# A new order of the first pieces, and short matmuls of zeros on TensorE, in a fused cross-attention and maxout kernel

## The chip, the core and the metric

The kernel runs on one core of a Trainium2 chip. Five engines take part: TensorE (PE in the profile; its weight loads are listed apart as PEld) multiplies matrices and writes only to PSUM, an on-chip memory of eight banks; VectorE (DVE), ScalarE (ACT) and GpSimd (POOL) do casts, copies, exponentials and sums; SyncE (SP) issues nearly all transfers between HBM and the on-chip memory SBUF, which then run on 16 DMA engines. Every engine works through its own instructions in the order in which they were written, and waits where an operand or a buffer is not ready. The metric is the device time of one execution in microseconds (us).

## The reference

`x` is (8, 8, 512, 64): batch, head, row, depth. `state` is (8, 8, 32, 64). Both are read in float32.

```python
scores = scale * x @ state^T;    a  = softmax(scores);   xread = a @ state
scores2 = scale * state @ x^T;   a2 = softmax(scores2);  sread = a2 @ x
y = concatenate([xread, sread], axis=rows)       # heads side by side: (8*544, 512)
out = maximum(y @ w1, y @ w2) @ w_out            # w1, w2: 512x1024, w_out: 1024x512
```

The output is (4352, 512) in float32.

## The kernel before

The kernel writes the maximum as `y @ w2 + relu(y @ (w1 - w2))`. For a batch b the matrix `y` is `a` times a block-diagonal state, so the weights are first multiplied with the state of the batch: `sw` = state times `wd = w1 - w2` (columns 0 to 1023) and state times `wwo = w2 @ w_out` (columns `w`). Then, for each batch,

- `l1.b.f` (line 332): two matmuls give 128 of the 1024 hidden columns, `re` takes the maximum with zero (lines 325, 327);
- `l2.b.c.q` (line 346): for each of four row groups c the hidden columns of the quarter q (two f) are multiplied with `w_out`; `l2.b.c.o` (line 341) adds the part by `wwo`; `le` copies the sum out and `store` writes it.

Before this come, for a batch: the load of `x` in two halves (`ldx.b.g`, 512 KB each), casts to bfloat16 (`ce`, `cb`), the transposes of `x` (on PE `xt`, copied out of PSUM by `xte`; for later batches by a transposing transfer, `xtd`), the scores `sc` (line 240), their exponential `exp` (line 248, on ACT), the sums `red` (line 252), the division `mul` (line 256), the transposes of `a` (on PE `at`, copied by `ate`; later by the transfer `atd`), and the reading of the state by x, `sr`, `sre`, `srt`, `srte` (line 280). `S` transposes the state (loads `ldS`, cast `cS`, copies `Se`; for batches 2 to 7 by the transfer `Sd` after the masked casts `mS`).

The weights are loaded in pieces, `ldw1.k`, `ldw2.k` and `ldwo.q`. A piece k of w1 and w2 is a range of columns and of 128-row tiles, listed in `PIECES`: all are 512 KB. `cw2` casts a piece of w2, `w2` transposes it on PE (line 405), `w2e` copies it out of PSUM; `sub.k.h` subtracts half of a piece of w2 from w1 (line 417); `cwo` casts a piece of `w_out`. `ww.i.q` (line 460) accumulates `wwo` for the row tile i over the column quarter q, and `wwe` copies it out. `CHUNKS[b]` says in which column ranges `sw` is made for the batches 0 and 1.

Until the loop over the batches 2 to 6 begins (line 573), the order on every engine is the list `ORDER`, written out by hand token by token. `name>V`, `>A`, `>P` put a token on DVE, ACT or POOL; `name@i` or `@i,j` puts a PE token into the PSUM bank i. A token with neither is a transfer, issued by SP (the state of batch 0, `ldS.0.1`, by ACT). `idle.9@0` is nine matmuls of zeros (line 426). PE's tokens up to the loop hold batches 0 and 1 whole, and the scores and `sw` of batch 2. In the loop, `cast_b(b+2)` on POOL and `xt_dma(b+2)` on SP stand ahead of the division `mul` and `at_dma` of batch b+1; `RELEASE` gives the order in which the loop takes over the banks. A buffer `big[k]` holds in turn the pieces and batches that `slot` lists: `x4` takes the place of the left half of w2.

```python
PIECES = [(0, 512, 0, 2), (0, 512, 2, 4), (512, 1024, 0, 2), (512, 1024, 2, 4)]   # columns, row tiles
```

## Time and profile before

| | |
|---|---|
| time, three runs | median 151.17 us (151.1 to 151.3) |
| the profiled execution | 150.94 us, its span 149.0 us |
| mean clock granted to TensorE | 0.989 |
| busy: PE, DVE, ACT, POOL | 138.1, 83.3, 66.1, 53.0 us |
| moved by DMA | 29.44 MB, mean 198 GB/s |
| PE's share of the chain that ended last | 81%, DMA 10% |

How to read the rows that follow. A row of the timeline or of the chain of waits begins with its start and its length in us from the start of the span, then the engine, the line of the program, the operation, what it writes and reads, and how many instructions were merged (x8); in brackets stands how long the engine was idle before and what it waited for. In a row of the view by stretches stand the stretch, its length, and for PE, PEld, DVE, ACT and POOL the busy time with the number of instructions; then the clock granted to PE, the mean share of the DMA engines, and GB/s. Rows on SPq are transfers being issued; the length is the issue, not the transfer. In the two rows of slices each digit is the busy share, or the clock, in tenths for a fortieth of the span.

### The profile page before, as it was taken

To read this page: it belongs to the slowest core of one execution; us is meant where nothing else is said; L and a number is where in the kernel's file an instruction comes from. 1 tells how busy PE (TensorE), PEld (TensorE's weight loads), DVE (VectorE), ACT (ScalarE), POOL (GpSimd) and SP (SyncE) were. 2 spreads that over 40 slices of the span, in tenths; PEclk is the share of its full clock that TensorE was granted. 3 is DMA by queue.
4 is the path that set the end of the run, shared out by engine and by line. 5 is a ranking of instruction groups with operands and counts; after the bars stand their busy time and mean duration, and the time that the engine had idled before them with its cause. 6 is when DMAs were issued, how large, how long until landed. Compare 5 with 4: busy or idle time off the path is not lost.

```text
span 149.0 us, 3067 instructions
## 1 busy us (share of the span) xinstructions
PE 138.1 (93%) x1205; PEld 68.9 (46%) x1224; DVE 83.3 (56%) x163; ACT 66.1 (44%) x120; POOL 53.0 (36%) x81
## 2 busy tenths in 40 slices
PE   6846979999999999999999999999999999999990
...
PEclk9987999999999999999999999999999999999999
...
GB/s 137 255 396 362 370 387 378 283 342 93 189 246 200 106 248 297 129 208 230 235 145 290 234 114 189 264 282 145 70 31 255 7 66 141 145 0 96 115 140 80
DMA packets 36063, 29.44 MB, mean 198 GB/s; under 512 B 23120, under 2 KB 31568, under 8 KB 35152
## 3 DMA queue, kind: packets, MB, share of 16 engines
...
q10 hardware_dynamic: 272, 0.07, 0.2%
...
## 4 chain that ended last, share of the span: by engine, by line
PE 81%; DMA 10%; SPq 3%; DVE 1%; issue 1%; POOL 1%; ACT 0%
PE bank L346 38%; PE bank L332 17%; PE bank L341 9%; DMA big<-in_moe_w_out_dram 7%; PE bank L309 4%; PE bank L460 3%; DMA big<-in_x_dram 3%; SPq L155 3%; PE bank L365 2%; PE bank L375 2%; PE bank L240 2%; PE bank L280 1%; PE bank L373 1%; DVE wd L417 1%; POOL wo L103 1%
## 5 line engine op out<-in xcount | busy, mean ns | idle before, releaser
L346 PE MATMUL bank<-wo,r 128*128 128x512 bf16 (+1 forms) x259 | 61.4, 372 | 0.5
L346 PEld LDWEIGHTS <-r 128*128 128x128 bf16 x264 | 25.4, 98 | 28.5 <-issue 0.3
L99 ACT COPY big<-bank 128x512 f32<-128x512 f32 (+1 forms) x17 | 9.7, 573 | 47.1 <-PE bank L346 47.1
L332 PE MATMUL bank<-at,sw 128*128 128x512 bf16 x126 | 30.0, 379 | 0.1
L256 POOL TENSOR_TENSOR a<-e,er 128x512 bf16<-128x512 bf16 x16 | 16.7, 1065 | 36.3 <-ACT e L248 16.0
L327 DVE TENSOR_SCALAR r<-bank 128x512 bf16<-128x512 f32 x29 | 20.0, 691 | 15.9 <-PE bank L332 15.5
L325 ACT ACTIVATE r<-bank 128x512 bf16<-128x512 f32 x35 | 21.2, 608 | 8.2 <-PE bank L332 8.0
L101 DVE CAST sw<-bank 128x512 bf16<-128x512 f32 x24 | 15.3, 685 | 9.4 <-PE bank L309 9.3
L103 POOL CAST xe<-big 128x512 bf16<-128x512 f32 x28 | 16.4, 620 | 10.0 <-DMA big<-in_x_dram 10.0
L332 PEld LDWEIGHTS <-sw 128*128 128x128 bf16 x128 | 12.0, 98 | 14.0 <-issue 0.2
L101 DVE COPY big<-bank 128x512 f32<-128x512 f32 (+1 forms) x16 | 10.5, 654 | 13.6 <-PE bank L346 11.2
L341 PE MATMUL bank<-sw,at 128*128 128x512 bf16 (+1 forms) x56 | 17.1, 372 | 0.3
L103 POOL CAST xb<-big 128x1024 bf16<-128x1024 f32 x12 | 12.3, 1041 | 12.1 <-issue 11.4
L252 DVE TENSOR_REDUCE sums<-e 128x16 f32<-128x512 bf16 x16 | 10.6, 664 | 4.5 <-ACT e L248 4.4
L99 ACT CAST sw<-bank 128x512 bf16<-128x512 f32 x24 | 12.7, 599 | 0.2
L248 ACT ACTIVATE e<-bank 128x512 bf16<-128x512 f32 x16 | 9.0, 595 | 4.9 <-PE bank L240 4.5
L460 PE MATMUL bank<-wo,w2m 128*128 128x512 bf16 x30 | 7.8, 379 | 1.9 <-ACT w2m L99 1.2
L341 PEld LDWEIGHTS <-at 128*128 128x128 bf16 x66 | 5.7, 97 | 5.3
L240 PEld LDWEIGHTS <-xt 128*128 128x128 bf16 x128 | 5.1, 98 | 2.6 <-DVE xt L101 0.7
L240 PE MATMUL bank<-sbd,xt 128*128 128x64 bf16 x128 | 5.5, 193 | 0.6 <-DVE xt L101 0.6
L309 PE MATMUL bank<-wd,sbd 64*32 64x512 bf16 x128 | 5.8, 382 | 0.3 <-DVE sbd L101 0.2
L101 DVE COPY w2m<-bank 128x1024 bf16<-128x1024 bf16 (+1 forms) x4 | 2.8, 689 | 5.1 <-PE bank L375 4.1
...
## 6 DMA issues: line engine op xcount, KB each, us to landing
big<-in_x_dram SPq DMA_DIRECT2D x14, 512.0 KB, 5.1
...
big<-in_moe_w_dram SPq DMA_DIRECT2D x8, 512.0 KB, 10.2
big<-in_moe_w_out_dram SPq DMA_DIRECT2D x4, 512.0 KB, 10.3
...
out_dram<-big SPq DMA_DIRECT2D x1, 512.0 KB, 2.6
...
```

The costliest lines, as they stand in the source:

```text
L99: nc.scalar.copy(o, i)
L101: nc.vector.tensor_copy(o, i)
L103: nc.gpsimd.tensor_copy(o, i)
L240: nc.tensor.matmul(pv[:, c, kk], xt_s[b % 2][:, c, k, :], sbd[:, b, k, :], start=(c == 0 and kk == 0), stop=(c == NC - 1 and kk == 1))
L256: (nc.gpsimd if eng == "P" else nc.vector).tensor_mul(e_view(a_s[b % 2], hh), e_view(e_s[b % 2], hh), er_s[b % 2][:, hh].unsqueeze(3).to_b ...
L309: nc.tensor.matmul(pg[g][32 * i:32 * i + 32, 0:n], sbd[64 * g:64 * g + 64, b, i, 32 * g:32 * g + 32], rhs, start=True, stop=True)
L325: nc.scalar.activation(out=o, in_=p, func=ACTF.Relu)
L327: nc.vector.tensor_scalar(o, p, scalar1=0.0, scalar2=None, op0=ALU.max)
L332: nc.tensor.matmul(p, sw_s[b % 3][:, g, f * 128:(f + 1) * 128], at_s[b % 3][:, g].rearrange("p c t -> p (c t)"), start=(g == 0), stop=(g = ...
L341: nc.tensor.matmul(p[:, lo:hi], at_s[b % 3][:, g, c, :], sw_s[b % 3][:, g, FF + lo:FF + hi], start=(start and g == 0), stop=(stop and g == 1))
L346: nc.tensor.matmul(p[:, lo:hi], r_s[b % 2][:, f, c * 128:(c + 1) * 128], wo[:, f, lo:hi], start=(start and j == 0), stop=(stop and j == le ...
L460: nc.tensor.matmul(p, w2t[:, f, i, :], wo[:, f, :], start=(first and f % 2 == 0), stop=(last and f % 2 == 1))
```

## The change

The new `PIECES` cuts the left half of w1 and w2 into two column quarters with all four row tiles, in place of two halves of the row tiles; the right half keeps its two pieces. `CHUNKS` for batch 0 makes `sw` in three ranges. The loads come in the order: state of batch 1, x0, x1 (right half of the heads first), w2.0, w1.0, wo.0, w2.3, w2.1, wo.1, w1.1, wo.2, wo.3, w2.2, w1.2, w1.3, then x2, x3.1, the state of batches 2 to 7, x4.1, x3.0. The transfers `xtd.3` and `ldx.4.0` stand behind `atd.2`. The remaining tokens of `ORDER` are put in another order, with other engines and banks in places, to go with these loads. `idle` takes a width; a new token `fill.n@i` is one matmul of zeros with 256 columns. There are 24 of them, and `idle.9` stands behind `xt.1.0`. `RELEASE` follows the new banks. What is computed stays the same.

```diff
--- before.py
+++ after.py
@@ -16,40 +16,42 @@
 
 
 
-PIECES = [(0, 512, 0, 2), (0, 512, 2, 4), (512, 1024, 0, 2), (512, 1024, 2, 4)]
-
-CHUNKS = [[(0, 512), (512, 1024)], [(0, 512), (512, 1024)]]
+PIECES = [(0, 256, 0, 4), (256, 512, 0, 4), (512, 1024, 0, 2), (512, 1024, 2, 4)]
+
+CHUNKS = [[(0, 256), (256, 512), (512, 1024)], [(0, 512), (512, 1024)]]
 
 ORDER = """
-ldx.0.0 ldS.0.1 idle.9@0 ldx.0.1 ldw2.2 ldw2.3 ldwo.3 ldw1.3 ldw1.2 ldS.1.2 ce.0.0>V ce.0.1>P ldx.1.1 cS.0.1>V ldx.1.0
-S.0.1@0 xt.0.0@1 Se.0.1.0>V Se.0.1.1>A ce.0.2>P ce.0.3>A xte.0.0>V xt.0.1@0 ldwo.2 sc.0.0@1 xte.0.1>V exp.0.0>A
-cw2.2>P ldw2.1 sc.0.1@0 red.0.0>V exp.0.1>A w2.2@1 mul.0.0>P cw2.3>A sr.0@0 red.0.1>V ldw2.0 mul.0.1>P sre.0>V w2.3@2
-cwo.3>A ldwo.0 w2e.2>V srt.0@0 at.0.0@3 srte.0>A sub.3.0>V w2e.3>A ldwo.1 sub.3.1>V ldw1.0 ate.0.0>A ww.2.3@2
-sub.2.0>V ldw1.1 at.0.1@1 cS.1.2>A ww.3.3@3 ww.1.3@0 sub.2.1>V ate.0.1>A ldS.2.8 S.1.2@4 sw.0.1@1,5 Se.1.2.1>V
-ce.1.3>A Se.1.2.0>V ce.1.2>P sw.1.1@4,6 swe.0.1.1>V ww.0.3@7 swe.0.1.0>A swe.1.1.0>V xt.1.1@5 swe.1.1.1>A ce.1.1>P
-l1.0.7@1 ce.1.0>A xte.1.1>V l1.0.4@6 l1.0.6@4 re.0.7>A re.0.4>V cwo.2>P xt.1.0@5 re.0.6>A sc.1.1@1 l1.0.5@6 xte.1.0>V
-exp.1.1>A ww.3.2@3 re.0.5>A sc.1.0@1 red.1.1>V ww.1.2@0 exp.1.0>A ww.2.2@2 cw2.1>V ww.0.2@7 l2.0.1.2@1 mul.1.1>P
-ldx.3.1 red.1.0>V w2.1@6 cw2.0>A l2.0.2.2@5 mul.1.0>P w2e.1>V l2.0.2.3@5 l2.0.1.3@1 cwo.0>V w2.0@6 at.1.1@4 ww.2.0@2
-w2e.0>V ldx.2.1 ww.3.0@3 cwo.1>P ate.1.1>V ww.0.0@7 ww.1.0@0 sub.0.1>V ldx.2.0 ww.3.1@3 at.1.0@4 ldx.3.0 sub.0.0>V
-ww.0.1@7 wwe.3>A ww.1.1@0 sub.1.1>P ate.1.0>V wwe.0>A ww.2.1@2 wwe.1>V l1.1.7@7 wwe.2>A sr.1@4 sub.1.0>V re.1.7>A
-sw.0.w@2,0 sre.1>V sw.0.0@3,6 swe.0.w.1>A l1.1.5@7 swe.0.w.0>V l1.1.6@4 swe.0.0.1>A mS.1>P l1.1.4@0 re.1.5>A re.1.6>V
-l2.0.0.2@6 re.1.4>A l2.0.1.o@1 swe.0.0.0>V ce.3.2>P sw.1.0@4,7 mS.0>A sw.1.w@3,0 ce.3.3>P swe.1.0.1>V l2.0.0.3@6
-swe.1.w.1>A cb.3.1>P Sd l1.0.0@2 swe.1.0.0>V l1.0.1@7 swe.1.w.0>A re.0.0>V l2.0.3.2@4 cb.2.1>P re.0.1>A l2.0.2.o@5
-l1.1.1@2 ce.3.0>P l2.0.1.0@1 re.1.1>V l1.0.2@7 cb.2.0>P l1.1.3@3 re.0.2>V l2.0.3.o@4 re.1.3>A ce.3.1>P xtd.2 l1.1.0@2
-ce.2.1>P l2.0.3.0@4 re.1.0>A srt.1@3 l2.0.0.0@6 ldx.4.0 cb.3.0>P srte.1>V l1.0.3@2 l2.0.0.o@6 re.0.3>A ce.2.2>P
-l2.0.3.3@4 xtd.3 l1.1.2@2 ce.2.0>P l2.0.1.1@1 re.1.2>A ce.2.3>P l2.1.3.2@3 le.0.1>V l2.1.3.3@3 l2.1.3.1@3 l2.1.3.0@3
-l2.1.2.2@1 ldx.4.1 l2.1.0.o@2 sc.2.1@7 l2.0.3.1@4 exp.2.1>A sc.2.0@0 l2.0.0.1@6 exp.2.0>A red.2.1>V l2.1.0.0@2
-le.0.3>A l2.1.0.3@2 red.2.0>V mul.2.1>P l2.1.0.2@2 l2.1.2.3@1 le.0.0>V l2.1.2.o@1 mul.2.0>P l2.1.0.1@2 l2.0.2.0@5
-le.1.0>A atd.2 l2.1.2.1@1 l2.0.2.1@5 l2.1.3.o@3 le.0.2>A l2.1.2.0@1 le.1.3>V sw.2.1@5,2 store.0 le.1.2>A sw.2.0@6,4
-swe.2.1.0>V sw.2.w@3,0 swe.2.1.1>A sr.2@1 swe.2.0.0>V l2.1.1.3@5 swe.2.w.1>A l2.1.1.o@5 sre.2>V swe.2.0.1>A l2.1.1.2@5
-l2.1.1.1@5 swe.2.w.0>V srt.2@1 l2.1.1.0@5 srte.2>V le.1.1>A
+ldS.1.2 ldS.0.1 fill.18@0 ldx.0.0 fill.12@1 fill.11@0 ldx.0.1 fill.14@1 fill.21@0 fill.16@1 ldx.1.1 fill.10@0 fill.5@1
+ldx.1.0 fill.2@0 fill.7@1 fill.4@0 ldw2.0 cS.1.2>P ldw1.0 cS.0.1>V S.0.1@0 fill.15@1 fill.0@2 Se.0.1.1>V Se.0.1.0>A
+fill.23@1 ce.0.1>A ce.0.0>P ldwo.0 fill.19@2 fill.20@1 xt.0.0@2 ldw2.3 ce.0.2>V ce.0.3>A ldw2.1 S.1.2@1 Se.1.2.0>A
+Se.1.2.1>V xt.0.1@0 xte.0.0>A fill.22@1 xte.0.1>V ldwo.1 ce.1.2>P ce.1.3>A sc.0.1@0 ldw1.1 fill.17@2 fill.1@1 xt.1.1@3
+exp.0.1>A fill.3@1 sc.0.0@2 xte.1.1>V ce.1.1>A ce.1.0>P exp.0.0>A red.0.1>V sc.1.1@3 fill.6@1 ldwo.2 xt.1.0@0
+exp.1.1>A idle.9@1 red.0.0>V mul.0.1>P ldwo.3 xte.1.0>A ldw2.2 mul.0.0>V cw2.0>A sub.0.0>P red.1.1>V sc.1.0@0 fill.9@1
+ldw1.2 exp.1.0>A w2.0@3 at.0.0@1 sub.0.1>V at.0.1@0 w2e.0>A sr.1@2 cwo.0>P ldw1.3 red.1.0>V sw.0.0@4,5 sr.0@6
+ate.0.1>A ldx.2.1 fill.8@3 swe.0.0.0>A swe.0.0.1>V mul.1.0>P ww.0.0@0 cw2.3>A ate.0.0>V ww.2.0@5 sre.0>V l1.0.0@1
+mul.1.1>P ww.1.0@4 cw2.1>A re.0.0>V l1.0.1@6 ldx.2.0 at.1.1@3 sre.1>V re.0.1>A w2.1@1 cwo.1>P ww.3.0@7 ate.1.1>A
+w2e.1>V ldx.3.1 w2.3@2 at.1.0@3 ww.1.1@4 sub.1.1>V w2e.3>A srt.1@1 ww.3.1@7 sub.1.0>V ww.0.1@0 ate.1.0>A ww.2.1@5
+cwo.2>V srte.1>A sw.0.1@3,2 ldS.2.8 sw.1.0@1,6 swe.0.1.1>A ww.3.2@7 swe.1.0.1>V swe.0.1.0>A l2.0.0.0@2 cwo.3>P
+swe.1.0.0>A l1.0.2@6 l1.0.3@1 re.0.2>A ww.2.3@5 cw2.2>V re.0.3>A ww.3.3@7 w2.2@6 wwe.3>V ww.2.2@5 w2e.2>A l1.1.2@1
+sub.2.0>V l1.1.0@7 sub.2.1>V re.1.2>A l1.1.3@6 ww.0.3@0 re.1.3>A re.1.0>V l1.1.1@1 wwe.2>A ww.1.2@4 sub.3.1>V ldx.4.1
+ww.0.2@0 re.1.1>A sub.3.0>V ww.1.3@4 wwe.0>A l2.1.2.1@1 wwe.1>V ce.2.3>P sw.0.2@5,7 ldx.3.0 sw.1.1@0,6 cb.2.1>P
+swe.0.2.1>V swe.0.2.0>A sw.1.w@4,3 l2.1.2.0@1 swe.1.1.1>A swe.1.1.0>V srt.0@7 cb.2.0>P l1.0.5@5 swe.1.w.0>A l1.0.4@6
+swe.1.w.1>V l1.1.6@0 srte.0>A ce.2.0>P xtd.2 re.0.4>A re.0.5>V l2.0.3.0@7 ce.3.2>P l2.1.1.o@3 re.1.6>A sw.0.w@5,6
+ce.3.3>P l1.1.4@0 swe.0.w.1>A swe.0.w.0>V mS.1>P l1.1.5@4 re.1.4>V mS.0>A l1.1.7@5 l2.0.3.1@7 re.1.5>V re.1.7>A
+l1.0.7@0 l2.0.2.2@6 re.0.7>A cb.3.1>P Sd l2.1.0.2@5 l2.1.2.2@1 l2.0.2.0@6 ce.2.1>P l2.1.2.3@1 ce.3.0>P l1.0.6@0
+ce.3.1>P l2.1.2.o@1 re.0.6>A l2.0.2.o@6 le.1.2>V cb.3.0>P l2.0.2.1@6 l2.0.1.3@0 ce.2.2>P l2.0.3.2@7 l2.1.0.o@5
+l2.0.0.1@2 l2.0.0.3@2 l2.0.3.o@7 l2.1.1.0@3 l2.0.0.2@2 sc.2.1@1 l2.1.1.3@3 exp.2.1>A sc.2.0@4 l2.0.3.3@7 exp.2.0>A
+red.2.1>V l2.0.2.3@6 le.0.3>A l2.0.1.1@0 red.2.0>V mul.2.1>P l2.0.0.o@2 le.0.2>A l2.1.3.3@7 le.0.0>A l2.1.1.2@3
+mul.2.0>P sr.2@6 l2.1.0.1@5 sre.2>V atd.2 l2.1.3.2@7 l2.0.1.o@0 l2.1.1.1@3 xtd.3 l2.1.0.0@5 le.1.1>A l2.1.0.3@5
+l2.1.3.o@7 le.1.0>A sw.2.0@3,6 sw.2.1@2,4 ldx.4.0 swe.2.0.1>V sw.2.w@5,1 swe.2.1.0>A l2.0.1.2@0 swe.2.1.1>V l2.1.3.0@7
+swe.2.w.0>A l2.1.3.1@7 swe.2.w.1>A swe.2.0.0>V srt.2@5 l2.0.1.0@0 le.1.3>A srte.2>V le.0.1>V store.0
 """
 
 LATE = 2
 
 WHOLE = (7,)
 
-RELEASE = [7, 2, 6, 0, 4, 3, 1, 5]
+RELEASE = [6, 2, 4, 1, 3, 5, 7, 0]
 
 
 @with_exitstack
@@ -420,10 +422,10 @@
     def wo_cast(q, eng):
         copy(eng, wo[:, 2 * q:2 * q + 2, :], half("o", q // 2)[:, q % 2 * 2:q % 2 * 2 + 2, :])
 
-    def idle(n, ring):
+    def idle(n, ring, w=512):
         p = bank(ring)
         for j in range(n):
-            nc.tensor.matmul(p, wz[:, 0:128], wz, start=True, stop=True)
+            nc.tensor.matmul(p[:, 0:w], wz[:, 0:128], wz[:, 0:w], start=True, stop=True)
 
     nc.vector.memset(wz, 0.0)
     nc.vector.memset(ones, 1.0)
@@ -479,7 +481,7 @@
         sre=("sr", lambda p, b, e: sr_ev(p, b)), srte=("srt", sr_cp), re=("l1", l1_ev), w2e=("w2", w2_ev))
     oth = dict(
         ldS=load_s, ldx=load_x, ldw2=lambda k: load_w(2, moe_w2, k), ldw1=lambda k: load_w(1, moe_w1, k), ldwo=load_wo,
-        idle=idle, cS=s_cast, mS=lambda z, e: s_mask(z, LATE, B, e), Sd=lambda: s_dma(LATE, B), ce=cast_e, cb=cast_b, xtd=xt_dma,
+        idle=idle, fill=lambda k, r: idle(1, r, 256), cS=s_cast, mS=lambda z, e: s_mask(z, LATE, B, e), Sd=lambda: s_dma(LATE, B), ce=cast_e, cb=cast_b, xtd=xt_dma,
         atd=at_dma, red=lambda b, h, e: red(b, h), mul=mul, cw2=w2_cast, sub=w_sub, cwo=wo_cast, ww=ww_mm, l2=l2_mm,
         wwe=lambda i, e: copy(e, wwo[:, i, :], open_[f"ww{i}"]), le=lambda b, c, e: l2_out(b, c, open_[f"l2{b}{c}"], e),
         Se=lambda lo, hi, j, e: s_ev(done[f"S.{lo}.{hi}"], lo, hi, j, e), store=store,
```

## The prediction

> **What bounds the kernel now.** The page first, its busy time and its slices:
>
> ```profile
> PE 138.1 (93%) x1205; PEld 68.9 (46%) x1224; DVE 83.3 (56%) x163; ACT 66.1 (44%) x120; POOL 53.0 (36%) x81
> PE   6846979999999999999999999999999999999990
> PEclk9987999999999999999999999999999999999999
> ```
>
> TensorE (PE) is busy for 93% of the span; its slices are below nine tenths only in five of the first six and in the last, and its clock dips to 7 in the fourth. Then the view by stretches, and from the timeline the first `l1` group of the loop over the batches:
>
> ```profile
> 31.30:54.66 23.36, 23.03 (x184) 10.63 (x188) 12.53 (x27) 11.96 (x21) 13.29 (x17) 1.00 0.80 205
> 54.66:149.00 94.34, 89.75 (x757) 44.17 (x767) 49.35 (x97) 37.40 (x72) 25.37 (x32) 1.00 0.59 154
> ```
> ```profile
> 54.66 3.62 PE L332 MATMUL bank<-at,sw 128*128 128x512 bf16 x16
> ```
>
> From 54.66 on PE is busy 89.75 of 94.34 us, so I let the loop take the same time whenever it starts. The question is when PE gets there. The chain of waits gives the price of each kind of PE work when nothing waits.
>
> ```profile
> 23.86 0.45 PE bank L405 x8
> 52.06 0.36 PE bank L280 x32
> 58.28 0.47 PE bank L240 x16
> 68.67 3.45 PE bank L332 x16
> 76.91 0.77 PE bank L309 x24
> ```
>
> ORDER holds 144 matmuls of 512 columns (32 `ww`, 32 `l1`, 80 `l2`) at 3.45/16, 31.05 us; 87 transposes at 0.45/8, 4.9; 48 score matmuls at 0.47/16, 1.4; three `sr` at 0.36, 1.1; 72 `sw` matmuls at 0.77/24, 2.3. Sum 40.8. So PE loses 54.66 - 40.8 = 13.9 us before the loop, and the change can gain only in those. By 17.0 it has done 45 transposes (2.5), two score groups (0.5), one `sr`, two `sw` (0.5) and five matmuls of `ww` (1.1), together 4.9: 12.1 us are lost up to there, 1.8 after.
>
> What is late at first are the loads: the first instruction that uses a piece starts when it has landed.
>
> ```profile
> 4.50 0.43 DVE L101 CAST xe<-big 128x512 bf16<-128x512 f32 x1 [2.21 <-DMA big<-in_x_dram]
> 4.84 0.70 DVE L101 CAST sb<-sf 128x256 bf16<-128x256 f32 x1
> 6.21 0.61 POOL L103 CAST xe<-big 128x512 bf16<-128x512 f32 x1 [0.82 <-DMA big<-in_x_dram]
> 9.13 1.04 POOL L103 CAST wb<-big 128x1024 bf16<-128x1024 f32 x1 [2.30 <-DMA big<-in_moe_w_dram]
> 10.43 1.05 ACT L99 CAST wb<-big 128x1024 bf16<-128x1024 f32 x1 [0.90 <-DMA big<-in_moe_w_dram]
> 16.32 0.61 POOL L103 CAST xe<-big 128x512 bf16<-128x512 f32 x1 [4.13 <-DMA big<-in_x_dram]
> 18.86 0.61 POOL L103 CAST xe<-big 128x512 bf16<-128x512 f32 x1 [1.93 <-DMA big<-in_x_dram]
> 20.21 1.04 POOL L103 CAST wo<-big 128x1024 bf16<-128x1024 f32 x1 [0.74 <-DMA big<-in_moe_w_out_dram]
> 28.50 1.26 POOL L417 TENSOR_TENSOR wd<-big,big 128x512 bf16<-128x512 f32 x1 [1.82 <-DMA big<-in_moe_w_dram]
> ```
>
> The same view cut finer gives, at the end of each row, the clock that PE was granted, the DMA share and the GB/s moved:
>
> ```profile
> 0.00:3.04 3.04, 1.77 (x5) 0.67 (x6) 1.19 (x3) 1.49 (x2) 1.52 (x20) 1.00 0.32 83
> 3.04:6.45 3.41, 3.10 (x15) 1.37 (x14) 1.26 (x3) 0.17 (x1) 1.03 (x2) 1.00 1.00 292
> 6.45:9.86 3.41, 1.70 (x28) 1.12 (x26) 2.62 (x5) 1.90 (x4) 1.11 (x2) 1.00 0.96 339
> 9.86:13.27 3.41, 3.04 (x53) 2.46 (x53) 1.95 (x7) 2.40 (x4) 2.33 (x3) 0.50 1.06 389
> 13.27:16.68 3.41, 2.01 (x23) 1.05 (x24) 3.03 (x7) 2.84 (x6) 0.36 (x1) 1.00 1.10 348
> 17.00:18.00 1.00, 1.00 (x19) 0.76 (x12) 0.85 (x2) 0.88 (x2) 0.00 (x0) 1.00 1.05 382
> ```
>
> **The change part by part.** *Loads.* Most pieces are 512 KB, and the bytes up to the last weight are the same in both orders, so I let the k-th piece land when the k-th landed before. Between the rows I go by equal steps: 1.47 for the four from 10.43 to 16.32, 1.38 for the six from 20.21 to 28.50. On SP the small state load of batch 1 now goes ahead of x0, one issue of 0.4 to 0.5 us: x0 at 4.9 and 6.4. Then x1 near 9.25 and 10.6 (it came at 16.3 and 18.8), w2.0 11.9, w1.0 13.4, wo.0 14.8, w2.3 16.3, w2.1 18.8, wo.1 20.2, w1.1 21.6, wo.2 23.0, wo.3 24.3, w2.2 25.7, w1.2 27.1, w1.3 28.5. The quarter pieces move runs of 1 KB, as x does, in place of 2 KB. No row times such a W load; by the rates just shown, 382 GB/s while x1 was on its way, 348 to 389 ahead of it, four pieces of 0.52 MB could differ by 0.6 us. I take 0 (382 is nearest), and keep 0.6 for the range; a gain has no reason.
>
> *Zeros.* `idle.9` goes from the head to behind `xt.1.0`; 24 `fill`s of 256 columns come in, 11 ahead of `S.0.1`. The nine are one row of the timeline now:
>
> ```profile
> 1.27 4.02 PE L426 MATMUL bank<-wz 128*128 128x512 bf16 x9 [1.27 <-DVE ones L429]
> ```
>
> The nine zeros took 0.43 each against 0.216 later, so PE began at half rate though the clock column says 1.00. By the rows cut finer PE is granted half from 9.86 to 13.27, after 3.41 us with 1.70 busy, and full again after 3.04 busy; 2.01 busy kept it. A fill thus costs 0.21 at half rate, 0.11 at full. The 11 run from 1.27 to 3.6; PE then waits for the cast of S0, now first on DVE: 4.7 to 5.4 (it began at 4.84, behind x0's cast). From 5.5 on five fills, then `xt.0.0`, `S.1.2` and `xt.0.1` at half rate (0.9, 0.2, 0.9) with a fill, then the scores keep it about 70% busy, so I take full rate from about 10, ahead of `idle.9`. The fills end before the inputs of what stands behind them are there, and cost nothing. Only `idle.9` is near: from 12.6, 9 x 0.216 bring it to 14.55, while `w2.0` waits for its cast until 14.9. Without that cover the nine would cost 1.9, at half rate 3.8. Behind it in PE's queue wait `sc.1.0`, on which ACT's `exp.1.0` depends, and `w2.0`. (The Trainium skill, "TensorE: Matmul & The Clock Gate", section "What's actually happening", has a free-running window of 3413 ns; the 3.41 us here agree. It would let the moment of full rate differ between executions.)
>
> *The stage up to the first `ww`.* ACT sets it, by these durations, of which the next may overlap some 0.07:
>
> ```profile
> 6.57 0.62 ACT L99 CAST xe<-big 128x512 bf16<-128x512 f32 x1
> 7.95 0.60 ACT L248 ACTIVATE e<-bank 128x512 bf16<-128x512 f32 x1 [0.76 <-PE bank L240]
> 13.15 1.11 ACT L99 COPY w2m<-bank 128x1024 bf16<-128x1024 bf16 x1
> ```
>
> In its order, with starts: `Se` 6.15 (after `S.0.1` and DVE's half), `ce.0.1` 6.45, so that `xt.0.0` begins on PE at 7.1 (before: 5.8), `ce.0.3` 7.0, `xte.0.0` 8.7, `ce.1.3` 9.7, `exp.0.1` 10.4, `ce.1.1` 10.95, `exp.0.0` 11.5, `exp.1.1` 12.25, `xte.1.0` 12.85, `cw2.0` 13.85, `exp.1.0` 14.95, `w2e.0` 15.6, `ate.0.1` 16.65 to 17.25: almost without a gap. The 1.11 is also my price for `xte` on ACT (no row; DVE took 0.4 less for such a copy, the other end). So `ww.0.0` starts at 17.3. PE has then done 52 transposes, four scores, two `sr` and half an `sw`: 4.7 us. Lost so far: 12.6, 0.5 more than before.
>
> *17.3 to the late weights.* Now PE has work in hand: 26 pairs of `ww`, `l1` and `l2` at 0.43 (11.2), 32 transposes (1.8), one and a half `sw` (0.4), 13.5 with `srt`, up to `sw.0.2`. Walking the queues with the landings above I find 0.5 us of waits (`sw.1.0` for the bank that `srte.1` empties, `l1.0.2` for `swe.1.0.1`). The two last subtractions stand on DVE behind `re.1.0` and go from 29.4 to 30.7, after w1.3 at 28.5, so that `sw.0.2` starts at 31.3 with 0.6 to spare. After it stand 46 pairs of matmuls (19.8), seven `sw` (1.8), two scores, `sr`, two `srt`: 22.6. With 0.3 of waits at `sw.1.w` and behind (before: 23.36 - 23.03 in that stretch) the loop starts at 54.2.
>
> ```profile
> sbd<-sb SPq DMA_TRANSPOSE x1, 4.1
> ```
>
> On SP the state load S.2.8 moves behind x2 and x3.1; it lands near 34, its transpose is issued at 37 and takes 4.1, and the scores of batch 2 come at 44.6: covered by 3.5 us.
>
> A subtraction on DVE costs 0.64, but 1.18 beside POOL:
>
> ```profile
> 27.02 1.28 DVE L417 TENSOR_TENSOR wd<-big,big 128x512 bf16<-128x512 f32 x2
> 29.89 2.21 POOL L200 TENSOR_SCALAR sb<-sf,mask 128x768 bf16<-128x768 f32 x1
> 30.16 1.18 DVE L417 TENSOR_TENSOR wd<-big,big 128x512 bf16<-128x512 f32 x1
> ```
>
> DVE's order (two reductions, `mul.0.0`, a reduction) brings `sub.0.1` to 15.3, while `cwo.0` runs on POOL until 16.05; I take 1.18, to 16.5. The Trainium skill, "SBUF — State Buffer", section "Who interferes with whom", says the second of two such instructions "fully blocks"; here DVE was done at 31.34 while POOL ran to 32.10, so the trace does not bear that out. By the rule `sub.0.1` would end at 16.7 and the loop start some 0.15 later.
>
> *Sum.* Lost: 12.6 + 0.5 + 0.3 = 13.4 against 13.9; 54.2 - 54.66 = -0.45 us. On the profiled execution's 150.94 (span 149.0 and 1.94 around it) that is 150.5; its own time is 0.23 below the median of 151.17, so on the median 150.7.
>
> **The rivals.** *The zeros do not bring the clock in time* (the change does not do what it says). If full rate comes only at 13.27, as 70% busy lies between the 2.01 that kept it and the 3.04 that brought it, the transposes and scores of 7 to 13 take twice as long, `idle.9` runs 13.7 to 15.65, `ate.0.1` ends at 18.2 and the first `ww` starts 0.95 later: 151.65. If `idle.9` itself ran at half rate, 13.7 to 17.5, the stage would end 3.2 later: 153.9. For it: half rate at the start and a hole from 3.6 to 5.5. Against: 3.04 of 3.41 was enough.
>
> *Late x4.* In the new order `xtd.3` and `ldx.4.0` stand behind `atd.2` on SP, which waits for POOL's last `mul`.
>
> ```profile
> 39.09 1.25 SPq L155 DMA_DIRECT2D big<-in_x_dram  x1
> 40.46 3.81 SPq L218 DMA_TRANSPOSE xt<-xb  x1
> 49.38 1.24 SPq L261 DMA_TRANSPOSE at<-a  x1
> 56.00 4.75 SPq L218 DMA_TRANSPOSE xt<-xb  x1
> big<-in_x_dram SPq DMA_DIRECT2D x14, 512.0 KB, 5.1
> at<-a SPq DMA_TRANSPOSE x6, 3.1
> ```
>
> `atd.2` at 48.9, `xtd.3` 50.1 to 53.9, x4.0 issued 54.4, landed 59.5; two casts of 1.04 on POOL to 61.6, ahead of the third batch's `mul`; `xt_dma(4)` holds SP to 66.4; `at_dma(3)` lands at 69.5, where its `l1` is due 14.0 after the loop's start, at 68.2 (68.67 - 54.66 before). A wait of 1.3: 152.0. It decides only if x4.0 lands after some 58.2; with `xtd.3` issued in 1.3 us it lands at 57 and costs nothing.
>
> *No difference.* Up to 17.3 the change loses 0.5. If the loads of the quarter pieces are 0.4 to 0.6 late, the gain that follows only pays for both: 151.1.
>
> **How the numbers follow.** A measurement of this kernel tells about 0.2% (0.3 us) from no change. Forecast 0.46 (its own range 149.9 to 150.85), no difference 0.14, clock late 0.20 (half-rate `idle.9` 0.05 more), late x4 0.15. Faster 0.46, same 0.14, slower 0.40. The range takes in ACT's `xte` at DVE's price (two copies, 0.4 each, less: 149.9) and, above, both slower cases with 0.4 of slow loads, 152.4; beyond lies the half-rate `idle.9`.
>
> **What would show it.** Right: x1's casts near 9.5 and 10.9; granted clock full from about 10; the first L460 matmul near 17.3 with PE nearly gapless from there; the last subtraction done by 30.7; L332's run of 16 at 54.2. Wrong: clock at 0.5 beyond 10.5; PE gaps between 17 and 31 that end on loads, which would mean the pieces land later than before's; a gap before the L332 run of batch 3, near 68.

## The result, and the profile after

The changed kernel takes 151.91 us (median; 151.24 to 155.04), the kernel before beside it 151.08: a ratio of 1.0071, with a 95% interval of 1.0047 to 1.0096. Two later comparisons of the same two kernels (e8 and e15 below) gave 1.0042 (1.0012 to 1.0073) and 1.0060 (1.0028 to 1.0092). So it is about 0.6% slower, where 0.3% faster was forecast: the time lies inside the stated range, but it moved the other way. (The ratios and their intervals leave out executions more than 1.5% above the fastest of their kernel, the medians take in all, so a ratio need not be the quotient of two medians.) The profiled execution took 152.14 us, its span 150.3.

The page of the changed kernel, its busy time, and PE's slices and clock:

```profile
PE 143.1 (95%) x1255; PEld 72.5 (48%) x1255; DVE 80.2 (53%) x157; ACT 71.0 (47%) x129; POOL 53.1 (35%) x80
...
PE   6689999999999999999999999999999999999990
...
PEclk9999999999999999999999999999999999999999
```

PE is busier than before, 143.1 us against 138.1, in a longer span. Part of the 5.0 more are the zeros and work at half rate, so "busy" is no gain here. The view by stretches, cut as in the prediction, with the columns that it had:

```profile
3.04:6.45 3.41, 2.22 (x11) 1.01 (x9) 0.52 (x2) 0.88 (x2) 1.01 (x2) 1.00 1.03 331
6.45:9.86 3.41, 2.79 (x25) 2.16 (x26) 1.35 (x3) 2.21 (x4) 0.61 (x1) 1.00 1.08 352
9.86:13.27 3.41, 3.26 (x38) 2.85 (x36) 1.75 (x4) 2.09 (x4) 0.68 (x2) 1.00 1.09 360
55.89:150.30 94.41, 90.39 (x769) 44.33 (x767) 49.96 (x98) 37.18 (x72) 27.42 (x34) 1.00 0.58 171
```

The loop over the batches takes 94.41 us from its first `l1` to the end of the span, 94.34 before: that the loop moves as a whole was right, and nearly all of the loss of this execution lies ahead of it. The timeline of PE says where. In this kernel every line number is higher by 2 (the zeros L428, transposes of x L227, `sw` L311, `ww` L462, `l1` L334):

```profile
1.27 2.53 PE L428 MATMUL bank<-wz 128*128 128x256 bf16 x11 [1.27 <-DVE ones L431]
...
6.47 1.03 PE L227 MATMUL bank<-ident,xe 128*128 128x128 bf16 x8 [0.38 <-POOL xe L105]
...
10.38 1.06 PE L227 MATMUL bank<-ident,xe 128*128 128x128 bf16 x8
...
12.85 1.06 PE L227 MATMUL bank<-ident,xe 128*128 128x128 bf16 x8
13.70 2.50 PE L428 MATMUL bank<-wz 128*128 128x512 bf16 x9
...
18.58 1.04 PE L462 MATMUL bank<-wo,w2m 128*128 128x512 bf16 x4
...
32.41 0.92 PE L311 MATMUL bank<-wd,sbd 64*32 64x512 bf16 x16
...
55.89 3.62 PE L334 MATMUL bank<-at,sw 128*128 128x512 bf16 x16
```

Eight transposes of x take 0.61 at full rate. At 10.38 and 12.85, where the forecast had full rate, they take 1.06. The nine zeros of `idle.9` take 2.50; at full rate throughout such a row takes 2.10 (e1 below). The 0.40 more are two zeros at half rate, 0.43 instead of 0.216 each, so PE becomes full near 13.70 + 0.86 = 14.6 (the clock column says 1.00 all the while, as it did over the slow start of the kernel before). The first `ww` begins at 18.58, not at 17.3, and the loop at 55.89, not at 54.2.

Between the two stands ACT, which the forecast had "almost without a gap". Here it stood idle for PE 0.74, 0.82, 0.16, 0.47 and 0.57 us between 9.5 and 17 (in e1 below, with the rate up early, 0.22 in all). Three of the rows, `exp.0.0`, `xte.1.0` and `exp.1.0`, forecast at 11.5, 12.85 and 14.95:

```profile
12.12 0.60 ACT L250 ACTIVATE e<-bank 128x512 bf16<-128x512 f32 x1 [0.82 <-PE bank L242]
...
13.95 1.01 ACT L101 COPY xt<-bank 128x1024 bf16<-128x1024 bf16 x1 [0.47 <-PE bank L227]
...
16.47 0.60 ACT L250 ACTIVATE e<-bank 128x512 bf16<-128x512 f32 x1 [0.57 <-PE bank L242]
```

The second place is near 30, on DVE and POOL:

```profile
30.16 2.50 DVE L419 TENSOR_TENSOR wd<-big,big 128x512 bf16<-128x512 f32 x2
...
30.62 2.94 POOL L105 CAST xb<-big 128x1024 bf16<-128x1024 f32 x2
```

DVE's last two subtractions take 2.50 together beside POOL's casts, not 1.28, and the two casts 2.94, not 2.02. Taken one by one the two engines' instructions end in turn: POOL at 30.68, DVE at 31.22, POOL at 32.12, DVE at 32.66, POOL at 33.56, so DVE each time 0.54 behind POOL and POOL 0.90 behind DVE. That looks like two engines taking turns, each waiting while the other works, and not like both running at a lower speed; in e8 below the last four ends lie 0.90, 0.54 and 0.90 apart again. `sw.0.2` at 32.41 waits for the second one: 0.92 where 0.62 is usual.

### The profile page after: what moved, and what is told of

The parts are those of the page before. It is cut to its first block, busy times and chain, and to the rows that moved or that the text cites. A ratio compares the mean times of both kernels' runs of the same rounds, so it can differ in the third digit from the quotient of the medians.

```text
span 150.3 us, 3148 instructions
## 1 busy us (share of the span) xinstructions
PE 143.1 (95%) x1255; PEld 72.5 (48%) x1255; DVE 80.2 (53%) x157; ACT 71.0 (47%) x129; POOL 53.1 (35%) x80
## 4 chain that ended last, share of the span: by engine, by line
PE 92%; DMA 3%; DVE 1%; POOL 0%; SPq 0%; issue 0%; ACT 0%
PE bank L348 37%; PE bank L334 19%; PE bank L343 10%; PE bank L462 5%; PE bank L311 5%; DMA big<-in_x_dram 3%; PE bank L242 3%; PE bank L227 3%; PE bank L367 2%; PE bank L377 2%; PE bank L428 2%; PE bank L282 2%; PE bank L407 1%; PE bank L375 1%; DVE xt L103 1%; PE bank L269 1%
## 5 line engine op out<-in xcount | busy, mean ns | idle before, releaser
L334 PE MATMUL bank<-at,sw 128*128 128x512 bf16 x128 | 30.1, 379 | 0.0
L258 POOL TENSOR_TENSOR a<-e,er 128x512 bf16<-128x512 bf16 x15 | 15.5, 1049 | 24.5 <-ACT e L250 11.6
L105 POOL CAST xb<-big 128x1024 bf16<-128x1024 f32 x12 | 13.2, 1114 | 26.6 <-issue 17.1
L103 DVE CAST sw<-bank 128x512 bf16<-128x512 f32 (+1 forms) x24 | 15.0, 673 | 13.7 <-PE bank L311 13.6
L105 POOL CAST xe<-big 128x512 bf16<-128x512 f32 x27 | 15.6, 611 | 10.2 <-DMA big<-in_x_dram 10.2
L343 PE MATMUL bank<-sw,at 128*128 128x512 bf16 (+1 forms) x66 | 19.1, 373 | 0.0
L334 PEld LDWEIGHTS <-sw 128*128 128x128 bf16 x128 | 12.2, 98 | 14.4 <-issue 0.5
L101 ACT CAST sw<-bank 128x512 bf16<-128x512 f32 (+1 forms) x26 | 13.1, 576 | 2.4 <-PE bank L311 2.4
L428 PE MATMUL bank<-wz 128*128 128x256 bf16 (+1 forms) x32 | 8.7, 412 | 1.3 <-DVE ones L431 1.3
L462 PE MATMUL bank<-wo,w2m 128*128 128x512 bf16 x32 | 8.5, 380 | 0.0
L242 PE MATMUL bank<-sbd,xt 128*128 128x64 bf16 x128 | 6.2, 202 | 0.7 <-DVE xt L103 0.6
L101 ACT COPY w2m<-bank 128x1024 bf16<-128x1024 bf16 (+1 forms) x4 | 3.6, 906 | 5.7 <-PE bank L377 4.6
```

What stands on the lines that cost most here:

```text
L101: nc.scalar.copy(o, i)
L103: nc.vector.tensor_copy(o, i)
L105: nc.gpsimd.tensor_copy(o, i)
L242: nc.tensor.matmul(pv[:, c, kk], xt_s[b % 2][:, c, k, :], sbd[:, b, k, :], start=(c == 0 and kk == 0), stop=(c == NC - 1 and kk == 1))
L258: (nc.gpsimd if eng == "P" else nc.vector).tensor_mul(e_view(a_s[b % 2], hh), e_view(e_s[b % 2], hh), er_s[b % 2][:, hh].unsqueeze(3).to_b ...
L334: nc.tensor.matmul(p, sw_s[b % 3][:, g, f * 128:(f + 1) * 128], at_s[b % 3][:, g].rearrange("p c t -> p (c t)"), start=(g == 0), stop=(g = ...
```

## The experiments

All of them are read in the same way. The last copy out of PSUM begins the same 90.42 us after the loop's start in every execution looked at (before 54.66 and 145.08, after 55.89 and 146.31); what comes after it, the last stores, varies by 1.3 (3.9 to the end of the span before, 4.0 after, up to 5.2 in e10). So an edit ahead of the loop is read best from the loop's start, and the time of an execution is that start plus 96.2 to 97.5; a difference in the end of the program has to be read apart from it. The medians tell whether the execution that was profiled was a typical one. No experiment leaves work of the reference out.

**e1, the zeros made denser.** The eleven fills of the head are replaced by a row of eight zeros of 512 columns, and five fills are added in the two holes of PE between 5 and 10.

```diff
-ldS.1.2 ldS.0.1 fill.18@0 ldx.0.0 fill.12@1 fill.11@0 ldx.0.1 fill.14@1 fill.21@0 fill.16@1 ldx.1.1 fill.10@0 fill.5@1
-ldx.1.0 fill.2@0 fill.7@1 fill.4@0 ldw2.0 ...
+ldS.1.2 ldS.0.1 idle.8@0 ldx.0.0 ldx.0.1 ldx.1.1
+ldx.1.0 ldw2.0 ...
-... fill.19@2 fill.20@1 xt.0.0@2 ...
+... fill.19@2 fill.20@1 fill.30@1 fill.31@1 xt.0.0@2 ...
-... fill.22@1 xte.0.1>V ... sc.0.1@0
+... fill.22@1 fill.32@1 fill.33@1 fill.34@1 xte.0.1>V ... sc.0.1@0
```

> The changed kernel, with zeros and no hole: nine... eight matmuls of 512 columns at the head in place of the 11 short ones (8 x 0.43 = 3.4 us, up to the first transpose at 4.6), two more short ones ahead of xt.0.0 and three more ahead of sc.0.1; all else as in the changed kernel. Theory 'late clock': PE stays busy from 1.27 on, gets the full rate by 8.1 (1.27 + two times 3.41), the zeros in the middle take 1.95 us instead of 2.50, the first ww starts at 17.4 to 17.8 instead of 18.58, the loop 0.7 to 1.1 us earlier, and the time falls by 0.7 to 1.1 us. Rival 'ACT's order and the landings set the stage, whatever PE's rate': the first ww within 0.3 of 18.6, the time within 0.3 us of the changed kernel.

Measured: 151.15 us, ratio 1.0006 (0.9970 to 1.0042). Rows of its timeline, PE and the one cast on ACT that matters:

```profile
6.30 0.61 PE L227 MATMUL bank<-ident,xe 128*128 128x128 bf16 x8
...
11.97 2.10 PE L428 MATMUL bank<-wz 128*128 128x512 bf16 x9
...
16.45 1.04 PE L462 MATMUL bank<-wo,w2m 128*128 128x512 bf16 x4
...
18.63 1.04 ACT L101 CAST wb<-big 128x1024 bf16<-128x1024 f32 x1 [1.02 <-DMA big<-in_moe_w_dram]
...
19.73 0.62 PE L407 MATMUL bank<-ident,wb 128*128 128x128 bf16 x8 [0.69 <-ACT wb L101]
...
54.22 3.62 PE L334 MATMUL bank<-at,sw 128*128 128x512 bf16 x16
```

The transposes run at full rate from 6.3, the first `ww` comes 2.1 us earlier than in the changed kernel, which is more than the theory had, and the loop starts at the 54.2 of the forecast. But a wait is new: PE stands 0.69 us for ScalarE's cast of w2.1, whose piece landed at 18.6. So the late rate is one cause, and behind it a landing is the next bound.

**e2, the new order with the zeros of the kernel before.** `idle.9` in the head, no other zeros.

```diff
-ldS.1.2 ldS.0.1 fill.18@0 ldx.0.0 fill.12@1 ...
+ldS.1.2 ldS.0.1 idle.9@0 ldx.0.0 ldx.0.1 ldx.1.1      (all other fill and idle tokens taken out)
```

> The new order with the zeros of before: nine matmuls of zeros at the head, none elsewhere. Theory 'late clock': the head brings the full rate once, near 6.5, but from 9 on PE is under half busy, the rate falls back and stays at half into the first ww, which take 0.86 a pair for up to 3.4 us; the time is that of the changed kernel within 0.7 us, with the loss now behind 17 and not ahead of it. Rival 'the zeros only hold PE up': the first ww starts at 17.5 or earlier and the kernel is 1 us or more faster than the changed one.

Measured: 152.15 us, ratio 1.0111 (1.0065 to 1.0157).

**e3, the new order with no zeros.** All `fill` and `idle` tokens taken out.

> The new order without any zeros. Theory 'late clock': half rate up to some 20 us, first ww at 18 to 18.6 and at 0.86 a pair, 0.8 to 2 us slower than the changed kernel. Rival 'the zeros only hold PE up': 0.6 us or more faster than the changed kernel.

Measured: 153.54 us, ratio 1.0199 (1.0152 to 1.0247). The first four matmuls of `ww` in e2 and, below, in e3, both from PE's timeline:

```profile
17.69 1.89 PE L462 MATMUL bank<-wo,w2m 128*128 128x512 bf16 x4
```
```profile
18.09 1.89 PE L462 MATMUL bank<-wo,w2m 128*128 128x512 bf16 x4
```

1.89 against 1.04: without enough zeros the first `ww` themselves run at half rate, and the loop starts at 55.59 and 56.10. The changed kernel's ratios are 1.0042 to 1.0071, so the zeros of the change are worth about 1.3% or more to the new order against none, and 0.4% or more against those of before, where the intervals still overlap. Nothing says that they cost time as a whole.

**e4, POOL held.** In the changed kernel a copy of two columns of `wd` on POOL makes its casts of batch 2 wait until DVE has finished the subtractions.

```diff
-... wwe.1>V ce.2.3>P sw.0.2@5,7 ...
+... wwe.1>V hold.0>P ce.2.3>P sw.0.2@5,7 ...
+    hold=lambda k, e: nc.gpsimd.tensor_copy(hz[:, 0:2], wd[:, 2, FF - 2:FF]),
```

> The changed kernel with one tiny copy on POOL ahead of the casts of x2, which reads what the last subtraction on DVE writes, so that POOL waits for it. Theory 'DVE and POOL in each other's way': the last two subtractions take 1.3 us together instead of 2.50, the last of the first sw group after them ends near 31.9 to 32.4 instead of 33.3, and the time falls by 0.3 to 0.6 us. Rival 'PE has work up to 32.4 anyway': the subtractions are faster, the loop starts within 0.1 us of 55.9, and the time is the same within 0.2 us.

Measured: 151.62 us, ratio 1.0046 (1.0018 to 1.0074). The subtractions take 1.28 for two again. But its loop start of 54.78 is not the work of the hold. With the same zeros as in the changed kernel, full rate was there much earlier (lines are higher by one more):

```profile
8.08 0.91 PE L228 MATMUL bank<-ident,xe 128*128 128x128 bf16 x8
...
10.24 0.61 PE L228 MATMUL bank<-ident,xe 128*128 128x128 bf16 x8
...
16.93 1.04 PE L463 MATMUL bank<-wo,w2m 128*128 128x512 bf16 x4
...
19.20 1.04 ACT L101 CAST wb<-big 128x1024 bf16<-128x1024 f32 x1 [1.11 <-DMA big<-in_moe_w_dram]
...
54.78 3.62 PE L335 MATMUL bank<-at,sw 128*128 128x512 bf16 x16
```

The transposes at 8.08 end sooner than the 1.03 of half rate, so the rate rose near 8.7. That those at 10.24 take 0.61 here and those at 10.38 took 1.06 there, with no instruction different ahead of them (the state and x landed 0.3 to 0.8 us later here), says that the moment of full rate is not fixed by the program. e8 and e15 look at that.

**e5 and e11, full rate in the old order.** The kernel before with eleven zeros of 256 columns in the hole ahead of `w2.2`; e11 is the same kernel again.

```diff
-... exp.0.1>A w2.2@1 mul.0.0>P ...
+... exp.0.1>A fill.11@2 w2.2@1 mul.0.0>P ...      (fill.n: n matmuls of zeros, 256 columns)
```

> The kernel before in its old order, with 11 zero matmuls of 256 columns put ahead of w2.2 (the 1.33 us in which TensorE waits there), and nothing else changed. It tells what the rate is worth in the old order, where TensorE ran at half rate from 9.86 to 13.27. Theory 'late clock, and only because the new order has earlier work to do': the transposes of w2.2 and w2.3 shrink from 1.03 to 0.61 us, but the old order then waits for landings and copies (1.19 us ahead of ww.2.3 at 14.54), so the loop starts at 54.3 to 54.7 instead of 54.66 and the time is that of before, ratio 0.997 to 1.001. Rival 'a full rate from 7 us on is worth about 1 us in any order': loop start 53.7, ratio 0.993 or less.

> The same kernel as e5. Its median there was 0.55% under that of before, but the one execution that was profiled took 151.46 us, its slowest but one of twelve, with a landing of x that TensorE waited 1.06 us for at 18.84 and a loop start of 55.26, so that profile can't show where the gain lies. Theory 'the rate is worth 0.8 us in the old order too': ratio 0.993 to 0.997 again, and in an execution of median time no wait at 18.8, the first at 21 shorter than the 0.70 of before, loop start 53.9 to 54.3. Rival 'chance of one chip': ratio 0.998 to 1.001, loop start 54.6.

Measured: 150.44 us, ratio 0.9945 (0.9914 to 0.9976), and then 150.80 us, ratio 0.9997 (0.9973 to 1.0021). The two intervals just touch; the gain of the first did not come back. Three rows of e11, from PE:

```profile
10.28 0.62 PE L405 MATMUL bank<-ident,wb 128*128 128x128 bf16 x8 [0.21 <-POOL wb L103]
...
15.16 1.91 PE L460 MATMUL bank<-wo,w2m 128*128 128x512 bf16 x4
...
54.87 2.32 PE L332 MATMUL bank<-at,sw 128*128 128x512 bf16 x10
```

The transposes of w2.2 take 0.62 where before they took 1.03, so there the zeros did their work. But in this execution the rate fell again behind them (granted clock 0.67 from 13.27 to 16.68 and 0.82 from there to 20.00), the first four `ww` in a row took 1.91 where before they took 1.03, and the loop starts at 54.87 against 54.66. In the profiled execution of e5 the rate stayed, but x1 landed late: PE waited 1.06 us for it at 18.84, and the loop started at 55.26. So neither profile shows what a lasting full rate is worth in the old order. That the rate was worth 0.8 us in any order was not borne out by the second run; whether there is a small gain stays open.

**e6, without the row in the middle.** The changed kernel without `idle.9`.

```diff
-exp.1.1>A idle.9@1 red.0.0>V ...
+exp.1.1>A red.0.0>V ...
```

> The changed kernel without the row of nine zero matmuls of 512 columns at 13.7 (idle.9), the short ones kept. In the changed kernel's profile the row took 2.50 us and ended at about 16.0, and sc.1.0, whose copied x was ready at about 13.9, stood behind it. Theory 'the row is what brings the full rate': without it the stretch from 13 to 16 has only some 1.5 of 3.41 us of work, the full rate comes 3 us later or more, the first ww run at half rate, loop start 55.9 or later, ratio to before 1.007 to 1.015. Rival 'the row delays real work, and the clock would come anyway': sc.1.0 1.5 to 2 us earlier, first ww at 17.5 or earlier, loop start 55.0 or earlier, ratio 1.003 or less.

Measured: 151.61 us, ratio 1.0001 (0.9973 to 1.0029). In its execution the rate rose within the transposes at 13.01, which took 0.81 for eight, and stayed; the first `ww` came at 18.09, the loop at 54.96. So the first theory, that the row brings the full rate, fell: the rate came without it. The rival is open. Its mechanism shows in a small part: behind the row ACT stood idle 0.57 us for `sc.1.0` in the first execution and 0.22 in e8 and e15, and that wait is gone here. The first `ww` was 0.5 to 0.7 earlier than in the first execution and in e8, but 0.6 later than in e15, and x had landed a microsecond earlier than in e8, which stood beside it (POOL's first cast of x at 6.01 and 7.03). That the ratio is 0.4% under e8's, and e10's below 0.15% under e12's, points the rival's way, within the intervals.

**e7, the dense zeros and POOL held.** The edits of e1 and e4 together.

> The denser zeros of e1 together with the held POOL of e4 (a copy of two columns of wd makes POOL's casts of xb begin after VectorE's last two subtractions). The clock comes full at about 6 us here as in e1, so what is left is the contention alone. In e1's profile the last two subtractions took 1.28 us beside other work and sw.0.2 stood at 31.18 with a small gap. Theory 'in e1 the subtractions were already undisturbed': loop start 54.2 as in e1, 0.0 to 0.1 earlier, time 151.0 to 151.2, ratio 0.999 to 1.001. Rival 'contention costs half a microsecond whatever the clock': loop start 53.7, time 150.6, ratio 0.997.

Measured: 151.90 us, ratio 1.0034 (1.0011 to 1.0056). The subtractions were undisturbed (1.28), as they were in e1 without the hold, and the loop started at 54.61: 35.59 after the cast of w2.1, which began at 19.02. In e1 it also started 35.59 after that cast. The hold had nothing to take away here, so no pair of runs prices the contention by itself.

**e8 and e15, the changed kernel again,** nothing edited, each beside the other kernels of its group.

> The changed kernel once more, nothing edited. It tells whether the moment at which TensorE reaches the full rate is fixed or differs between executions with the same zeros. In the first profile of it the 128-column transposes at 10.38 took 1.06 us for eight (half rate), the row at 13.70 took 2.50 us, and the loop began at 55.89; in e4 with the same zeros 0.61 us, 2.11 us and 54.95. Theory 'the moment differs with the chip's own window': transposes, row and loop start anywhere between these two, time 151.6 to 152.1, ratio 1.004 to 1.008. Rival 'the moment is fixed, and e4 was earlier through its edit': the same 1.06, 2.50 and 55.9 within 0.1.

> The changed kernel unedited, beside e13 and e14 on one chip. Theory: ratio 1.004 to 1.007 as the two times before, loop start 55.2 to 55.9, with x0.0 landing at 5.4 or later and the first ww at 17.5 to 18.8. Rival 'the losses seen were those of the first chips': ratio under 1.002.

Measured: 152.13 us, ratio 1.0042, and 151.84 us, ratio 1.0060. PE's timeline in e8, and below in e15 with the cast of w2.1:

```profile
11.64 1.06 PE L227 MATMUL bank<-ident,xe 128*128 128x128 bf16 x8
...
13.84 0.61 PE L227 MATMUL bank<-ident,xe 128*128 128x128 bf16 x8
...
18.77 1.04 PE L462 MATMUL bank<-wo,w2m 128*128 128x512 bf16 x3
...
55.70 3.62 PE L334 MATMUL bank<-at,sw 128*128 128x512 bf16 x15
```
```profile
8.63 0.95 PE L227 MATMUL bank<-ident,xe 128*128 128x128 bf16 x8
...
10.83 0.61 PE L227 MATMUL bank<-ident,xe 128*128 128x128 bf16 x8
...
17.52 1.04 PE L462 MATMUL bank<-wo,w2m 128*128 128x512 bf16 x4
...
19.70 1.04 ACT L101 CAST wb<-big 128x1024 bf16<-128x1024 f32 x1 [1.02 <-DMA big<-in_moe_w_dram]
20.79 0.62 PE L407 MATMUL bank<-ident,wb 128*128 128x128 bf16 x8 [0.72 <-ACT wb L101]
...
55.28 3.62 PE L334 MATMUL bank<-at,sw 128*128 128x512 bf16 x16
```

The three executions of one program had full rate near 14.6 in the first, near 12.8 in e8 (the eight scores at 12.70 took 0.47, which lies between the 0.61 of half rate and the 0.41 of full), and near 9.3 in e15 (the transposes at 8.63 took 0.95). The moment differs, as the first theory said. It does not decide alone: in e15 the rate came early, PE was at the transposes of w2.1 early, and waited there 0.72 us, for a piece that landed at 19.7. In e8 the subtractions beside POOL took 2.12 for two and `sw.0.2` did not wait for them.

**e9, e10 and e12: two variants of the dense kernel, and the dense kernel again.** e9 puts `ww.3.0` and the transposes of w2.3 ahead of those of w2.1; e10 leaves `idle.9` out of the dense kernel; e12 is e1's kernel.

```diff
 e9
-... re.0.1>A w2.1@1 cwo.1>P ww.3.0@7 ate.1.1>A w2e.1>V ldx.3.1 w2.3@2 at.1.0@3 ...
+... re.0.1>A ww.3.0@7 w2.3@2 w2.1@1 cwo.1>P ate.1.1>A w2e.1>V ldx.3.1 at.1.0@3 ...
 e10
-exp.1.1>A idle.9@1 red.0.0>V ...
+exp.1.1>A red.0.0>V ...
```

> e1's denser zeros, and TensorE's order changed at one place: ww.3.0 and the transposes of w2.3 go ahead of the transposes of w2.1. In the profiles of e1, e4 and e7, the three in which TensorE came early, it waited 0.69, 0.81 and 1.21 us there, for ScalarE's cast of w2.1, which landed at 18.6 to 19.1; the two moved groups take 0.43 and 0.45 us. Theory 'with the clock settled the new order is bound by the loads: w2.1, and right behind it wo.1': the wait for w2.1 goes, but ww.1.1 behind it then waits for POOL's cast of wo.1, which ended at 21.03 in e1 where ww.1.1 began at 21.45, so 0.3 to 0.4 of the wait is gained: loop start about 53.9 where e1 had 54.22, ratio 0.2% under e12's. Rival 'w2.1 alone bounds': loop start 53.5, ratio 0.5% under e12's. Rival 'no load bounds': no change.

> e1's denser zeros without the row of nine zero matmuls (idle.9). In e1 the row ran from 11.97 to about 13.9, with the full rate on since 6.3, and the copy that sc.1.0 behind it needs was ready at 13.2; but the next real work, the transposes of w2.0, waits for a ScalarE cast that ends at 14.1. Theory 'once the clock is up the row costs nothing': the same loop start as e1, 54.2, and no difference to e12 over 0.2%, unless the hole of 2 us lets the rate fall. Rival 'the row is only needed while the clock is late, and costs half a microsecond', as e6 against the changed kernel seemed to show (151.61 against 152.1): loop start 53.8, ratio 0.3% under e12's. Rival 'the hole loses the rate': transposes at 14.2 with 1.03 us for eight and first ww with 1.9 us for four, ratio 0.5% above e12's.

> The kernel of e1 again, beside e9 to e11 on one chip. Theory 'the head's holes are the changed kernel's loss': ratio 0.997 to 1.002, transposes at the full rate from the first ones on, first ww at 16.4 to 16.9, a wait of 0.5 to 1.2 us for w2.1 near 19.7, loop start 54.2 to 54.7. Rival 'e1 was a lucky chip': ratio 1.004 or more, as the changed kernel.

Measured: 151.37 us, ratio 1.0022 (1.0000 to 1.0043); 151.38 us, 1.0021 (0.9991 to 1.0051); 151.40 us, 1.0036 (1.0009 to 1.0062). Between the three there is no difference that can be told. e12, from PE and ACT:

```profile
19.49 1.04 ACT L101 CAST wb<-big 128x1024 bf16<-128x1024 f32 x1 [0.50 <-DMA big<-in_moe_w_dram]
20.59 0.62 PE L407 MATMUL bank<-ident,wb 128*128 128x128 bf16 x8 [1.32 <-ACT wb L101]
...
55.08 3.62 PE L334 MATMUL bank<-at,sw 128*128 128x512 bf16 x15
```

The ratio of 1.0036 lies between what the theory and its rival had, so e1's 1.0006 was in part luck. With the rate up from the first transposes on, PE waits 1.32 us for w2.1, which in e1 had landed 0.9 earlier. The swap of e9 took that wait away in its execution, but another of 0.32 us, for the copy of w2, came behind it, and the head there was late by itself (full rate only near 10, loop at 55.29): whether the swap is worth its 0.2% stays open. In e10 the hole of two microseconds did lose the rate, as one rival had it; that made PE later at the transposes of w2.1, where it then did not wait, and the loop started at 54.64, no later than in e12:

```profile
14.91 1.06 PE L269 MATMUL bank<-ident,a 128*128 128x128 bf16 x8
...
17.56 1.25 PE L462 MATMUL bank<-wo,w2m 128*128 128x512 bf16 x3
```

**e13 and e14: x first on the queue, and w2.1 loaded earlier.** e13 issues the state load of batch 1 behind the first piece of x; e14 also loads w2.1 before w2.3. Both have the dense zeros.

```diff
-ldS.1.2 ldS.0.1 idle.8@0 ldx.0.0 ldx.0.1 ldx.1.1
+ldS.0.1 idle.8@0 ldx.0.0 ldS.1.2 ldx.0.1 ldx.1.1      (cS.1.2>P moved behind ce.0.0>P)
 e14 besides
-... ldw2.3 ce.0.2>V ce.0.3>A ldw2.1 ...   ... ww.0.0@0 cw2.3>A ...   ... ww.1.0@4 cw2.1>A ...
+... ldw2.1 ce.0.2>V ce.0.3>A ldw2.3 ...   ... ww.0.0@0 cw2.1>A ...   ... ww.1.0@4 cw2.3>A ...
```

> e1's denser zeros, and the load of the state piece S.1.2 issued behind x0.0's first piece instead of ahead of it (POOL's cast of it behind the cast of x0.0), so that x is first on SP's queue as in the kernel before. In the new order's profiles x0.0 landed at 5.4 to 7.0, in before at 4.5. Theory 'the piece queued ahead costs x its 0.5 us of issue and the start of the stream': x0.0 at 4.5 to 5.2, first transposes of x at 5.2 to 5.9, first ww 0.5 us earlier than e1's 16.45 and e12's 16.71, but then a longer wait for w2.1, so loop start as in the dense ones, 54.2 to 55.1, and ratio 1.000 to 1.003. Rival 'the head alone bounds': loop start 53.7, ratio 0.998. Rival 'the late landing is chance of the stream's start': x0.0 at 5.4 or later again.

> e13, and the loads of w2.1 and w2.3 swapped in SP's queue, with ScalarE's casts of them; TensorE's order stays (w2.1 before ww.3.0 and w2.3). w2.1 then lands about 1.45 us earlier (17.0 to 17.9) and w2.3 where w2.1 did; w2.3's cast ends about 19.7 to 20.4, and its transposes stand 0.9 us behind w2.1's. Theory 'with the head settled the landings bound': the wait of 0.7 to 1.3 us ahead of w2.1 shrinks to under 0.3, what is left waits for wo.1 (cast done at 21.0) or w2.3, loop start 53.6 to 54.2, ratio 0.996 to 1.000. Rival 'the landings do not bound': as e13.

Measured: 151.77 us, ratio 1.0039 (1.0005 to 1.0072), and 151.91 us, ratio 1.0045 (1.0021 to 1.0070). First the stretch from 2.00 to 3.50 of the view by stretches (last two columns: DMA share and GB/s), in the kernel before, in the changed kernel and in e13:

```profile
2.00:3.50 1.50, 1.50 (x5) 0.58 (x4) 0.29 (x1) 0.30 (x2) 0.26 (x5) 1.00 0.94 285
```
```profile
2.00:3.50 1.50, 1.50 (x9) 0.94 (x7) 0.30 (x1) 0.29 (x2) 0.67 (x6) 1.00 0.68 153
```
```profile
2.00:3.50 1.50, 1.50 (x5) 0.57 (x4) 0.30 (x1) 0.30 (x2) 0.26 (x5) 1.00 0.77 246
5.50:6.50 1.00, 0.94 (x10) 0.86 (x11) 0.23 (x2) 0.35 (x2) 0.26 (x1) 1.00 0.87 215
```

In the changed kernel the stream begins at 153 GB/s (119 in e8, 108 in e15), in the kernel before at 285. The difference, (285 - 153) x 1.5 us = 0.2 MB, is 0.56 us at the 352 GB/s that follow, and 0.75 in e15. The kernel before has its own slow microsecond at 5.50 to 6.50, with 139 GB/s, after it issued the same small state load at 4.57 (there SP also issued nothing from 5.04 to 6.18); in e13 the start is quick, x0.0 is there for its cast at 4.75 instead of 5.80, and the slow part comes later, 215 GB/s at 5.50 (256 from 4.00 to 6.50, and 268 in e14). So in three places of the queue a slow stretch came behind the small load. That the load is its cause is the likeliest reading; no run leaves the load out. Put first, it has that stretch ahead of x, but behind it the stream is as late as ever:

```profile
18.62 1.05 ACT L101 CAST wb<-big 128x1024 bf16<-128x1024 f32 x1 [0.34 <-DMA big<-in_moe_w_dram]
...
54.22 2.97 PE L334 MATMUL bank<-at,sw 128*128 128x512 bf16 x13
```

w2.1 is cast at 18.62 in e13 as in e1, and the loop starts at 54.22 in both. In e14 PE no longer waited for w2.1, but 0.42 us at 26.35 for a cast on DVE, and the loop started at 54.26: a later wait took the place of the earlier one. Both medians lie 0.8 to 1.3 us above the profiled executions (151.0 and 150.64), which were among the quickest of their kernels, so these rows show what happens when all goes well; what the slower executions wait for was not seen. Neither kernel beats the one before.

## Why the prediction was wrong

*The step that failed* is in the part on the zeros: "then the scores keep it about 70% busy, so I take full rate from about 10, ahead of `idle.9`". In the profiled execution PE was busy for 2.79 of 3.41 us from 6.45 and for 3.26 from 9.86, more than I had assumed, and still ran at half rate until about 14.6. The price, from the rows: the first `ww` at 18.58 in place of 17.3, 1.3 us. I had this as the first rival, with a chance of 0.20 and 151.65 us. It named the rows nearly as they came (`idle.9` from 13.7, ending at 15.65; it began at 13.70 and ended near 16.05) and has the direction, though not the reason: it took a PE busy for 70% as too little, and PE was busier than that. The sentence that such a window "would let the moment of full rate differ between executions" stood in the prediction and was not used. In five executions with the same zeros ahead of it the rate came near 8.7 (e4), 9.3 (e15), 12.8 (e8), 13.4 (e6) and 14.6 us; I took one value near the early end, and the first execution had the latest. So that the rate came late in this profile is in part chance; but in e4 and e15, where it was in time, the loop still started at 54.78 and 55.28 and not at 54.2. (The Trainium skill, "TensorE: Matmul & The Clock Gate", section "What's actually happening", has the free-running window; the executions agree with a phase that the program does not set.) A phase alone moves the moment by less than one window of 3.41 us, though, and they lie 5.9 apart, so the holes in PE's work must count as well. What decides is not shown: the 3.41 us up to the change hold 2.84 us of work in e8, and in the first execution the 3.41 us from 7.71, one window ahead of the last, hold 2.82 and did not bring the rate.

*The sum of the others.* From the first `ww` to `sw.0.2` 14.0 was forecast and 13.83 measured, with the 0.5 of waits nearly absent because PE came late. From `sw.0.2` to the loop 22.9 was forecast and 23.48 measured; 23.04 in e1 and e15, so 0.44 of it goes with the contention of DVE and POOL. I had priced that at `sub.0.1`, by the row of 1.18 (it took 0.88 and ended at 16.48, as forecast), and not at the last two subtractions. By that one row of the kernel before, the prediction had also set aside that the second of two such instructions waits until the first is done. The ends in turn at 30.68 to 33.56 look as if it does; the row of the kernel before does not. So +1.3 - 0.2 + 0.6 = +1.7, which is 55.89 - 54.2. In e8 the same two ran beside POOL and cost next to nothing (23.10), so this term belongs to some executions only.

*What was right, and hid the next bound.* With the rate in time the loop does start at 54.2 (e1, e13). But that is the early end, and not the typical case. These executions came early enough to wait for w2.1:

| execution | first `ww` | cast of w2.1 begins | loop begins | difference |
|---|---|---|---|---|
| e1, dense | 16.45 | 18.63 | 54.22 | 35.59 |
| e4, POOL held | 16.93 | 19.20 | 54.78 | 35.58 |
| e7, dense, POOL held | 16.35 | 19.02 | 54.61 | 35.59 |
| e12, dense again | 16.71 | 19.49 | 55.08 | 35.59 |
| e15, changed kernel | 17.52 | 19.70 | 55.28 | 35.58 |

The loop begins 35.59 us after that cast, however early the first `ww` was. I had w2.1 land at 18.8, which gives 54.4; it landed at 18.6 to 19.7. The forecast's "x0 at 4.9" was too early for the same reason: its casts began at 5.42 to 7.03 in the new order (4.50 before), since what came ahead of x was not one issue alone but a slow start of the stream. The mean of the five is 54.8, where the kernel before has 54.66. So even with the zeros cured the new order has next to nothing to gain of the 0.45 us. That w2.1's landing sets the loop's start whenever PE comes early is shown by the five differences, and by e14, where w2.1 came earlier and the wait was gone; why the stream's slow start is longer in some executions than in others is not shown.

*What stays open.* Seven runs of kernels with dense zeros lie at ratios of 1.0006 to 1.0045, mean 1.0029, and three of the changed kernel at 1.0042 to 1.0071, mean 1.0058. By these means the late rate is worth some 0.3%, half of the loss. On one chip it is less sure: e7 is 0.08% under e8, e13 and e14 are 0.21% and 0.15% under e15, all within the intervals. The other half is not w2.1, which takes the gain away but does not make the kernel slower than before: in the seven profiles the loop starts at 54.22 to 55.29, mean 54.62, as early as before. What is longer there is the end of the program, from the last copy to the end of the span: 4.1 to 5.2 us, mean 4.5, against 3.9 in the kernel before and 4.0 and 4.2 in e5 and e11. With three profiles of the old order this may be chance; no run looked for the reason, and this half of the loss is unexplained.

*The rivals.* The late x4 fell: in the changed kernel it came when I said, and the wait did not follow.

```profile
59.47 2.02 POOL L105 CAST xb<-big 128x1024 bf16<-128x1024 f32 x2 [8.86 <-DMA big<-in_x_dram]
...
69.74 2.54 PE L334 MATMUL bank<-at,sw 128*128 128x512 bf16 x11
```

The third batch's `l1` starts 13.85 after the loop's start; 14.01 before. The transposing transfer of x4 was issued in 3.08 us, not the 4.75 that I had taken. The later loop is not the reason: in e1, where it starts at 54.22, these casts begin at 57.83 and the third batch again 13.85 after the loop's start. "No difference" had the loads of the quarter pieces late by 0.4 to 0.6; the stream ran at 352 to 375 GB/s in the stretches from 6.45 to 20 us (339 to 389 before), so the quarter pieces were not slow, and its start was.
